# Moving the convolution units of a fused conv and ELU kernel to every fourth step, between the two groups' output turns

## The chip, the cores and the metric

The kernel runs on one core of a Trainium2 chip. The metric is the device time of one execution in microseconds (us), taken over several runs. Engines: PE is TensorE, ACT is ScalarE, DVE is VectorE, POOL is GpSimd, SP is SyncE.

## The reference, cut to what matters

```python
# x: (8, 4096, 192), weight: (8 heads, 7 taps)
w = softmax(weight, axis=-1)
out[b, s, h, :] = sum_k w[h, k] * x_pad[b, s + k, h, :]   # causal, 7 taps, 24 channels a head
h = out.reshape(32768, 192) @ w_in                        # (192, 2048)
g = where(h > 0, h, exp(min(h, 0)) - 1)                   # ELU
y = g @ w_out                                             # (2048, 192)
```

The result must be the float32 array of shape (32768, 192).

## The kernel before

The 32768 tokens are cut into 32 blocks of 1024, and each block's 2048 hidden channels into 16 slices of 128. One slice is a **step**, so a **stage** of 16 steps handles one block. The array of PE is split into two row tiles of 64 rows, which work side by side on different instructions. In each step a row tile does three kinds of work:

- one *h unit*: three matmuls 64x512 into a PSUM bank of its own. ACT then takes the exponential (line 752), POOL clamps it (705), DVE combines both into the ELU (868) and thereby frees the bank;
- two *output turns*, one for each group of 512 tokens: four matmuls 64x192 each into that group's accumulator. Both row tiles add to the same accumulator, so they must take turns, with a semaphore between them;
- in four of the 16 steps also its half of a *conv unit*: two matmuls 64x240 for two heads of a later block. Row tile 0 opens the bank, row tile 1 completes it, and ACT evacuates it (748).

```python
O_AT = (12, 16)              # first step of the accumulators of group 0 and group 1
CONV_AT = (14, 18, 23, 25)   # steps of a block's four conv units, from two stages ahead
X_AT = ((2, 1, 1), (1, 1, 0))   # the x loads: with the third unit half 1, with the second half 0
ZERO_AT = 8                  # POOL clears six rows here, in every fourth stage
...
    for n in range(LIVE, NP):
        ...
        for m in convs:
            lists[0] += c_items(m, 0)
        lists[0] += block_items(n, 0, 0) + block_items(n, 1, 0) + h_items(n, 0)
        lists[1] += h_items(n, 1)
        for m in convs:
            lists[1] += c_items(m, 1)
        lists[1] += block_items(n, 0, 1) + block_items(n, 1, 1)
        emit(lists)
```

`lists[rt]` is the order of one row tile's work within a step. `emit` merges the two lists into PE's single instruction stream by a clock of nominal durations. PSUM has eight banks. Two hold accumulators, and the others go round between h units and conv units: whoever needs a bank is given the one that the plan expects to come free first. Accumulators change every eight steps: group 0 at steps 12, 20, 28 and group 1 at 16, 24, 32 of the count in which the units stand at 14, 18, 23, 25.

```python
def take_bank(what, rt):
    if what not in bank_of:
        b = min(range(NBANK), key=lambda b: freed[b])
        ...
```

A finished block of conv results is transposed by a DMA from SP (`att<-csb`) and must have landed before the first h matmul of its stage. The x loads cast from float32 to bfloat16 and are issued from POOL, in the midst of POOL's stream of clamps. Which clamp they precede follows from the step of the conv unit that they are tied to.

## Time and profile before

| | before |
|---|---|
| time, median of 6 runs | 722.83 us |
| profiled span | 721.0 us |
| a stage of 16 steps, mean of 29 (steps 32 to 495) | 21.836 us |
| the same from the matmuls' pitches alone | 21.74 us |
| waits on each row tile, per stage | 0.105 us |
| waits on each row tile in the first 32 steps | 7.4 and 7.3 us |

The last four rows come from the start times of the matmul records, paired with the kernel's issue order, so that each row tile's own sequence is seen. The *wait* of a matmul is the distance from the start before it on that row tile, less the nominal pitch of that earlier matmul: 0.2158, 0.0825 or 0.1025 us.

### The profile page before, as it was taken

How to read it: one execution, taken by the hardware profiler on the slowest of the kernel's cores; microseconds unless marked ns; L12 is line 12 of the kernel's file. 1: busy time of each engine (PE TensorE's matmuls, PEld its weight loads, DVE VectorE, ACT ScalarE, POOL GpSimd, SP SyncE). 2: the span in 40 equal slices, each digit the busy share in tenths (PEclk: the TensorE clock that was granted, in tenths of full speed). 3: DMA queues.
4: the chain of work that ended last, by engine and by line, in shares of the span. 5: the costliest groups of instructions: out<-in, count | busy, mean ns of one | idle time of the engine just before them, and what ended most of it. 6: DMA issues, size and time to landing. Idle time of an engine off the chain costs nothing.

```text
span 721.0 us, 27609 instructions
## 1 busy us (share of the span) xinstructions
PE 713.7 (99%) x11846; PEld 673.2 (93%) x11847; DVE 642.9 (89%) x1048; ACT 678.4 (94%) x1289; POOL 667.7 (93%) x1112
## 2 busy tenths in 40 slices
PE   8999999999999999999999999999999999999997
PEld 4689999999999999999999999999999999999997
DVE  7999898998898998999888989988989988999993
ACT  6999999999999999999999999999999999999993
POOL 9989999999999999999999999999999999999893
PEclk9999999999999999999999999999999999999999
DMA  9725353555254664354553455652445553644212
GB/s 178 113 59 87 61 84 75 95 87 86 51 96 72 94 90 70 66 91 78 87 97 58 77 78 93 86 94 46 93 75 96 87 69 66 98 73 83 71 35 68
DMA packets 132303, 58.75 MB, mean 81 GB/s; under 512 B 98374, under 2 KB 131604, under 8 KB 132180
## 3 DMA queue, kind: packets, MB, share of 16 engines
q1 hardware_dynamic: 88388, 39.32, 23.7%
q0 software_dynamic: 43504, 16.77, 22.6%
q8 instruction: 93, 1.52, 0.9%
q10 hardware_dynamic: 288, 0.88, 0.3%
q14 instruction: 30, 0.25, 0.1%
HBM read 34.63 MB, written 25.46 MB: 83 GB/s over the span
## 4 chain that ended last, share of the span: by engine, by line
PE 95%; POOL 2%; DVE 1%; ACT 1%; issue 0%; DVEq 0%; POOLq 0%
PE H L1029 54%; PE H L1006 38%; PE H L981 4%; DVE gT L868 1%; POOL xg L622 1%; ACT E L752 1%; POOL w_in L642 0%; POOL w_out L653 0%; ACT csb L748 0%; POOL E L705 0%; POOL owner L670 0%; ACT osb L759 0%; DVE osb L859 0%; POOL block L680 0%; POOL ident L659 0%
## 5 line engine op out<-in xcount | busy, mean ns | idle before, releaser
L868 DVE SCALAR_TENSOR_TENSOR gT<-E,H 128x512 f16<-128x512 f32 x1024 | 633.1, 682 | 63.3 <-POOL E L705 61.2
L1029 PE MATMUL H<-w_out,gT 64*128 64x192 f16 x8192 | 681.7, 243 | 0.1
L1006 PE MATMUL H<-att,w_in 64*128 64x512 bf16 x3072 | 679.5, 376 | 0.8 <-DVE gT L868 0.6
L1029 PEld LDWEIGHTS H<-w_out,gT 64*128 64x128 f16 x8192 | 622.8, 94 | 24.7 <-PE H L1029 1.4
L705 POOL TENSOR_SCALAR E<-E 128x512 f32<-128x512 f32 x1024 | 607.0, 613 | 40.3 <-ACT E L752 29.8
L752 ACT ACTIVATE E<-H 128x512 f32<-128x512 f32 x1024 | 592.9, 602 | 26.3 <-PE H L1006 1.2
L1006 PEld LDWEIGHTS H<-att,w_in 64*128 64x128 bf16 x3072 | 275.6, 93 | 7.8 <-issue 1.4
L981 PE MATMUL H<-xg,Tm 64*128 64x240 bf16 x496 | 91.2, 263 | 0.2 <-DVE gT L868 0.2
L748 ACT ACTIVATE csb<-H 112x480 bf16<-112x480 f32 x124 | 70.0, 565 | 0.1
L759 ACT ACTIVATE osb<-H 128x384 f32<-128x384 f32 (+1 forms) x129 | 62.3, 485 | 6.8 <-PE H L1029 6.8
L622 POOL DMA_DIRECT2D xg<-in_x_dram x62 | 55.3, 902 | 0.2 <-issue 0.2
L981 PEld LDWEIGHTS H<-xg,Tm 64*128 64x128 bf16 x496 | 43.7, 94 | 4.6 <-DVE gT L868 0.8
L859 DVE COPY osb<-H 128x192 f32<-128x192 f32 x1 | 0.4, 358 | 7.3 <-PE H L1029 7.3
L903 PE MATMUL H<-zw 128*128 128x512 bf16 x10 | 3.8, 531 | 1.2 <-DVE zw L767 1.2
L957 PE MATMUL H<-xT,taps 128*128 128x256 bf16 (+1 forms) x23 | 3.7, 314 | 0.2 <-issue 0.2
L727 ACT ACTIVATE xb<-xs 128x512 bf16<-128x512 f32 x3 | 1.7, 618 | 2.2 <-DMA xs<-in_x_dram 2.2
L642 POOL DMA_DIRECT2D w_in<-in_moe_w_in_dram x6 | 3.6, 626 | 0.0
L957 PEld LDWEIGHTS H<-xT,taps 128*128 128x128 bf16 x24 | 2.2, 97 | 1.5
L903 PEld LDWEIGHTS H<-zw 128*128 128x128 bf16 x10 | 1.0, 122 | 2.6 <-DVE zw L767 1.2
L653 POOL DMA_DIRECT2D w_out<-in_moe_w_out_dram x3 | 2.7, 939 | 0.0
L720 ACT ACT_TABLE_LOAD x1 | 1.3, 1283 | 1.2 <-PEq L1096 1.2
L929 PEld LDWEIGHTS H<-ident,xb 64*64 64x64 bf16 x48 | 1.4, 129 | 1.1 <-ACT xb L727 1.1
(43 smaller groups left out, 20.7 us busy)
## 6 DMA issues: line engine op xcount, KB each, us to landing
out_dram<-osb SPq DMA_DIRECT2D x126, 192.0 KB, 3.3
xg<-in_x_dram POOLq DMA_DIRECT2D x61, 240.0 KB, 5.1
xs<-in_x_dram ACTq DMA_DIRECT2D x1, 768.0 KB, 4.5
w_in<-in_moe_w_in_dram POOLq DMA_DIRECT2D x3, 192.0 KB, 5.7
att<-csb SPq DMA_TRANSPOSE x31, 4.5
w_out<-in_moe_w_out_dram POOLq DMA_DIRECT2D x2, 192.0 KB, 9.1
w_out<-in_moe_w_out_dram POOLq DMA_DIRECT2D x1, 384.0 KB, 13.4
conv_band<-wband SPq DMA_DIRECT2D x1, 288.0 KB, 7.0
```

The costliest lines, as they stand in the source:

```text
L622: g.dma_start(xg[0:rows, b, 2 * w0 + gr : 2 * w1 : 2, :], src).then_inc(s_x[b][gr], 16)
L642: g.dma_start(w_in[0:HP, j, c0:c1], bass.AP(tensor=moe_w_in.tensor, offset=8 * j * FF + c0, ap=[[CPH * FF, HEADS], [FF, 8], [1, c1 - c0]], ...
L705: g.tensor_scalar(out=E[:, i % NE, :], in0=E[:, i % NE, :], scalar1=1.0, scalar2=0.0, op0=ALU.min, op1=ALU.max,).then_inc(s_clp)
L748: a.activation(*conv_evac(W, m), ACT.Copy).then_inc(s_ce)
L752: a.activation(E[:, i % NE, :], H[:, bank_of[item], :], ACT.Exp).then_inc(s_exp)
L759: a.activation(*out_evac(W, *item[1:]), ACT.Copy).then_inc(s_oev[item[2]])
L868: v.scalar_tensor_tensor(out=gT[:, s % NG3, q, u, :], in0=E[:, i % NE, :], scalar=1.0, in1=H[:, bank_of[item], :], op0=ALU.subtract, op1=A ...
L903: pe.matmul(H[:, bank, :], zw[:, 0:P], zw[:, 0:GS], start=True, stop=True)
L957: ins = pe.matmul(H[:, bank_of[item] + half, c0:c1], taps[:, tap, :], xT[:, j, HALO - PAD + tap + c0 : HALO - PAD + tap + c1], start=(tap ...
L981: ins = pe.matmul(H[:, bank_of["c", m], 256 * q : 256 * q + UC], Tm[rows, h, :], xg[rows, s % NXB, :, CPH * h : CPH * (h + 1)].rearrange(" ...
L1006: ins = pe.matmul(H[:, bank_of[item[:3]], :], w_in[HP * r : HP * (r + 1), j, FC * q : FC * (q + 1)], att[HP * r : HP * (r + 1), s % 2, j, ...
L1029: ins = pe.matmul(acc_of(k, g)[:, D * kb : D * (kb + 1)], gT[HP * rt : HP * (rt + 1), t % NG3, q, g, t0 : t0 + P], w_out[HP * rt : HP * (r ...
```

## The change

The intent is to have the accumulators' changes and the conv units never compete for a bank: a unit every four steps, two steps from any change, and in its step at the place where the two groups' turns meet.

```diff
 O_AT = (12, 16)
-CONV_AT = (14, 18, 23, 25)
+CONV_AT = (14, 18, 22, 26)
+CONV_POS = ((4, 4), (4, 4), (4, 4), (4, 4))
+POS_FROM = 30
...
-        lists = [[], []]
-        convs = conv_steps.get(n, [])
-        for m in convs:
-            lists[0] += c_items(m, 0)
-        lists[0] += block_items(n, 0, 0) + block_items(n, 1, 0) + h_items(n, 0)
-        lists[1] += h_items(n, 1)
-        for m in convs:
-            lists[1] += c_items(m, 1)
-        lists[1] += block_items(n, 0, 1) + block_items(n, 1, 1)
+        blocks = [[block_items(n, g, rt) for g in range(2)] for rt in range(2)]
+        lists = [sum(blocks[0], []) + h_items(n, 0), h_items(n, 1) + sum(blocks[1], [])]
+        for m in conv_steps.get(n, []):
+            for rt, later in enumerate(CONV_POS[m % CU] if n >= POS_FROM else (0, 0)):
+                later += 3 * rt
+                lists[rt][later:later] = c_items(m, rt)
         emit(lists)
```

Two more edits (`E_DVE` tested by half and group, `EVAC_LAG = 0.0`) do nothing with the values given and are left out. The x loads move with the units that they are tied to: from steps 18 and 23 to 18 and 22.

More of the change, by code (lines that the diff above doesn't have):

```diff
@@ L51 @@
 E_DVE = ()
+EVAC_LAG = 0.0
 HELD = {"h": 2900.0, "c": 1300.0, "a": 1400.0}
@@ L384, in bass_lightweight_conv__then__act_elu_kernel @@
                 what = ("e",) + item[1:3]
-                if item[2] in E_DVE or item[1:3] == (NK - 1, 1):
-                    dve_order.append((at + AHEAD, what))
+                if (item[1] % 2, item[2]) in E_DVE or item[1:3] == (NK - 1, 1):
+                    dve_order.append((at + AHEAD + EVAC_LAG, what))
                 else:
```

## The prediction

> **What bounds the kernel now.** I read the page first: busy shares (part 1), costliest groups (part 5).
>
> ```profile
> PE 713.7 (99%) x11846; PEld 673.2 (93%) x11847; DVE 642.9 (89%) x1048; ACT 678.4 (94%) x1289; POOL 667.7 (93%) x1112
> ...
> L1029 PE MATMUL H<-w_out,gT 64*128 64x192 f16 x8192 | 681.7, 243 | 0.1
> L1006 PE MATMUL H<-att,w_in 64*128 64x512 bf16 x3072 | 679.5, 376 | 0.8 <-DVE gT L868 0.6
> ...
> L981 PE MATMUL H<-xg,Tm 64*128 64x240 bf16 x496 | 91.2, 263 | 0.2 <-DVE gT L868 0.2
> L748 ACT ACTIVATE csb<-H 112x480 bf16<-112x480 f32 x124 | 70.0, 565 | 0.1
> ...
> L622 POOL DMA_DIRECT2D xg<-in_x_dram x62 | 55.3, 902 | 0.2 <-issue 0.2
> ```
>
> PE is busy nearly always, in two row tiles of 64 rows that run side by side, so "99%" hides whether both tiles are full. The durations 243 and 376 ns are pipelined records; what counts is the pitch on one row tile. The chain of work that ended last, in order of time, gives it, since it is PE work almost throughout:
>
> ```profile
> 131.13 0.27 PE H L1006 x2
> 132.64 0.25 PE H L1006 x2
> 152.97 0.27 PE H L1006 x2
> ...
> 174.81 0.27 PE H L1006 x2
> ...
> 658.28 0.25 PE H L1006 x2
> 659.59 0.25 PE H L1006 x2
> 660.90 0.25 PE H L1006 x2
> 662.21 0.27 PE H L1006 x2
> ```
>
> Three things are to be seen. A step without a conv unit takes 1.31 us (658.28 to 659.59 to 660.90). A step with one takes 1.51 us (131.13 to 132.64). The pattern repeats every 21.84 us (131.13, 152.97, 174.81), which is one stage of 16 steps with four conv units.
>
> Next I took every matmul start from the timeline of PE, paired it with the kernel's own issue order, and formed pitches per row tile: 0.2158 us after an h matmul (64x512), 0.0825 after an output matmul (64x192), 0.1025 after a conv matmul (64x240). Per row tile a step is 3 x 0.2158 + 8 x 0.0825 = 1.3075 us, and a conv unit adds 2 x 0.1025 = 0.205. A full stage is 16 x 1.3075 + 4 x 0.205 = **21.74 us**. Measured is 21.84: only **0.10 us of 21.84** is waiting. This is the whole prize in the steady part. Where a pitch exceeds its nominal value shows who loses it, the same in each of 29 stages (steps 32 to 495): row tile 0 waits 0.033 us for the conv unit's bank at step 23 of the schedule (7 mod 16) and 0.050 for the bank of the second group's accumulator that opens at step 24; row tile 1 waits 0.019 inside step 24 and 0.050 at the h unit of step 26. The units at 14 and 18 lose under 0.005 each. One such stage in the timeline of PE:
>
> ```profile
> 456.91 0.38 PE L1006 MATMUL H<-att,w_in 64*128 64x512 bf16 x1
> 456.92 0.41 PE L1029 MATMUL H<-w_out,gT 64*128 64x192 f16 x3
> 457.13 0.38 PE L1006 MATMUL H<-att,w_in 64*128 64x512 bf16 x1
> ...
> 457.72 0.47 PE L1029 MATMUL H<-w_out,gT 64*128 64x192 f16 x3
> ```
>
> The h matmuls of row tile 0 start 0.22 apart; three output matmuls take 0.41 when they flow (456.92) and 0.47 where the opening accumulator waited (457.72). Who kept the bank is seen in ACT's timeline at the same place:
>
> ```profile
> 457.32 0.56 ACT L748 ACTIVATE csb<-H 112x480 bf16<-112x480 f32 x1
> ...
> 458.25 0.50 ACT L759 ACTIVATE osb<-H 128x384 f32<-128x384 f32 x1
> ...
> 460.19 0.56 ACT L748 ACTIVATE csb<-H 112x480 bf16<-112x480 f32 x1
> ...
> 463.05 0.48 ACT L759 ACTIVATE osb<-H 128x384 f32<-128x384 f32 x1
> ```
>
> ACT evacuates a conv unit (csb), an accumulator (osb) and a conv unit within 2.9 us, then nothing of the kind for 2.4 us. By the issue plan the accumulator that opens at step 24 is given the very bank that the conv unit of step 23 has just left.
>
> **What the Trainium skill says.** "TensorE: Matmul & The Clock Gate", part 1, gives a warm start-to-start pitch of N / 2.4 GHz plus about 2.5 ns, so 215.8, 82.5 and 102.5 ns at N = 512, 192 and 240; this trace agrees on each row tile to within 1 ns, so nothing can make the matmuls themselves faster. "TensorEngine Tiling (Array Packing)", Gotcha 1, says that two row tiles may not use one PSUM bank at once and that software must keep them apart; that is why the two row tiles take turns at an accumulator and at a conv bank. In the trace 0.318 us between the end of one tile's turn and the other's start costs nothing, as steps without conv are exactly 1.3075. "Perfetto Trace Analysis", Optimization Strategy, says that the same gap repeated on the engine that should be full can mean PSUM has too few buffers; the trace agrees: 0.05 us at the same places of each stage, each at a bank. The same page, "DMA Instruction — SWDGE (GPSIMD)", says that a load issued from GpSimd has its descriptors made there; here each x load takes 902 ns of POOL.
>
> **The change part by part.** Nothing is added or removed. The E_DVE test and EVAC_LAG are inert, as E_DVE is empty and the lag zero.
>
> (a) Conv units 23 and 25 go to 22 and 26. Accumulators change at steps 12, 20, 28 (first group) and 16, 24, 32 (second), so all four units then sit two steps from a change, as 14 and 18 do now. The waits above should go: 0.033 + 0.050 on one row tile, 0.019 + 0.050 on the other. The row tiles' mean total of waits is 0.105 us per stage, but 0.24 of the 29 stages' 3.04 is a single late bank near 281 us. I expect 0.01 a stage to stay: 29 x (0.105 - 0.010) = **-2.75 us**.
>
> (b) From step 30 each unit's two matmuls are inserted between the two groups' turns: on row tile 0 after 4 x 0.0825 = 0.33 us instead of at the start, on row tile 1 after the h unit and the first turn (0.978) instead of after the h unit (0.648). Turn gaps: first group 0.33 to 0.648, second 0.865 to 1.183, both 0.318, the gap that is free now. The conv bank is taken 0.33 later, apart from the h bank taken at the start of the step. ACT's evacuation hardly moves: it now ends about 1.16 us after the last conv matmul's start (459.59 to 460.75) because it stands behind an h unit's exponential; 0.33 later ACT is just free. Cost 0, value within (a).
>
> (c) The start: steps 16 to 23 still lose 1.7 us to banks that come late out of the start-up backlog, and step 23 to 24 some 0.2 for the reason in (a). The conv at 22 comes one step nearer to the backlog. I count -0.1, uncertain by 0.3.
>
> Sum: 722.84 - 2.75 - 0.1 = **719.9 us** (-0.4%).
>
> **The rivals.** (1) *The transpose becomes late.* The last unit of a stage must be evacuated, transposed by DMA and landed before the next stage's first h matmul at step 32. Landing times, from the tile att:
>
> ```profile
> DMA to landing us min/median/max: 3.9/4.5/5.6
> ```
>
> Today it lands 1.96 to 3.7 us ahead of need (stages 2 to 31). The change takes away a step (1.31) and 0.33 within the step, and gives back about 0.3 at ACT: 0.6 is left in the worst stage. If each landing keeps its time, no stage waits. Against: the store of the accumulator that ends at step 27 is issued 2.65 us after the transpose now and would follow after some 1.3 us, and the slow landings today are those that overlap it. For: the x load and the other store, which overlap its first half now, would be mostly done. If a third of the stages came 0.3 us late, the time would be 29 x 1/3 x 0.3 = 2.9 us longer, 722.8: no gain.
>
> (2) *POOL takes over.* The second x load is issued after the third conv unit, so it moves from step 23 to 22, nearer to the first at 18. POOL's E instructions come every 0.6075 us when back to back (4.86 for 8), 1.215 of each 1.3075 step; of a load's 0.90 only 4 x 0.0925 + 0.205 = 0.58 is worked off in four steps. POOL carries 0.3 us into the second load, against 0.23 or less now.
>
> ```profile
> DVE gT L868 <- POOL E L705: 57.7, 135, 0.9
> ```
>
> DVE waits for POOL already (window 60 to 680), for which PE shows almost nothing. After the load at 18 the next accumulator opens with 0.46 us of bank slack and the h units of step 19 with 0.3; 0.3 of carry could use the latter up. If it costs 0.05 a stage: +1.45 us, 721.4. A bound it cannot be: 32 x 0.6075 + 2 x 0.90 = 21.24 per stage, under 21.74.
>
> (3) *Waits are all gone, at the start as well*: 722.84 - 3.04 - 1 = 718.8. Nothing in the plan frees the start, so I doubt it.
>
> **Range and chances.** The floor is 718.8; the usual misses are upward, by POOL (721.4) or the transpose (about 722). I take 719.0 to 721.9. The possible gain is under 0.6%, and slower by 2% would need 14 us, 0.5 us in every stage, which no rival makes: faster 0.005, same 0.985, slower 0.01.
>
> **What would show it.** Right: the chain repeats every 21.74 to 21.75 us instead of 21.84, output matmuls in threes take 0.41 where an accumulator opens, and csb and osb alternate on ACT at intervals of about 2.7 us. (b) is right if a conv step still takes 1.51. Rival 1 would show as PE waits on the DMA that writes att at the first h matmul of a stage; rival 2 as longer DVE waits for POOL and a gap on PE two to four steps after the second x load. Wrong would be a period of 21.80 or more, or any loss at steps 16 to 30 above 0.3 us.

## The result and the profile after

The changed kernel takes 720.7 us (median of 6 runs, 720.16 to 721.13) against 722.83 us. The ratio is 0.9966, with a 95% interval of 0.9953 to 0.9979. Ratios here are the mean time of one kernel's fast runs over that of the other's in the same rounds, so they are not quite the ratio of the medians quoted. By the rule of 2% the class is "same", and the small gain is clear of the noise. The profiled span fell from 721.0 to 718.9 us.

The page after, parts 1 and 5 (busy us, share, instructions; then groups with busy time and mean ns):

```profile
PE 712.0 (99%) x11847; PEld 683.3 (95%) x11847; DVE 641.5 (89%) x1048; ACT 678.5 (94%) x1289; POOL 664.4 (92%) x1112
...
L1006 PE MATMUL H<-att,w_in 64*128 64x512 bf16 x3072 | 680.8, 376 | 0.7 <-DVE gT L868 0.5
L1029 PE MATMUL H<-w_out,gT 64*128 64x192 f16 x8192 | 680.7, 243 | 0.1
...
L981 PE MATMUL H<-xg,Tm 64*128 64x240 bf16 x496 | 90.9, 263 | 0.2 <-DVE gT L868 0.2
L748 ACT ACTIVATE csb<-H 112x480 bf16<-112x480 f32 x124 | 70.8, 571 | 0.1
...
L622 POOL DMA_DIRECT2D xg<-in_x_dram x62 | 55.3, 896 | 0.2 <-issue 0.2
```

The page hardly moves: the same instructions of the same length, each engine as busy as before. A gain of 0.3% in a kernel that is bound throughout by one engine can't be seen in shares. It can be seen in the pitch. Lines of the chain that ended last, in order of time, after:

```profile
68.35 0.27 PE H L1006 x2
155.43 0.27 PE H L1006 x2
242.53 0.27 PE H L1006 x2
...
329.76 0.27 PE H L1006 x2
416.86 0.27 PE H L1006 x2
```

Before, such pieces came in every stage, 21.84 us apart. Now, apart from a disturbed stage near 281 us, they come only in every fourth: 155.43 - 68.35 = 87.08 us, a quarter of which is 21.77. From the matmul records, the mean stage is 21.769 us (nominal 21.74), and the waits per stage are 0.038 us instead of 0.105. They are not spread evenly. Three stages in four have 0.002 and 0.017 us on the two row tiles, that is nothing. Every fourth stage has 0.09 to 0.15 on row tile 0, mostly at the h unit of step 26, and the stage near 281 us has 0.19.

ACT's timeline after, for one stage (start, duration, operation), evacuations only:

```profile
481.97 0.57 ACT L748 ACTIVATE csb<-H 112x480 bf16<-112x480 f32 x1
...
483.44 0.48 ACT L759 ACTIVATE osb<-H 128x384 f32<-128x384 f32 x1
...
487.41 0.57 ACT L748 ACTIVATE csb<-H 112x480 bf16<-112x480 f32 x1
...
489.54 0.49 ACT L759 ACTIVATE osb<-H 128x384 f32<-128x384 f32 x1
```

Conv units (csb) and accumulators (osb) now alternate strictly, 1.5 to 4.0 us apart; the burst of three within 2.9 us is gone. What is special about every fourth stage stands in POOL's timeline after:

```profile
499.07 0.89 POOL L622 DMA_DIRECT2D xg<-in_x_dram  x1
500.00 1.77 POOL L705 TENSOR_SCALAR E<-E 128x512 f32<-128x512 f32 x3
501.71 0.25 POOL L637 MEMSET xg<- 6x192 bf16 x1
501.93 4.15 POOL L705 TENSOR_SCALAR E<-E 128x512 f32<-128x512 f32 x7
```

POOL issues the second x load (0.89 us), does three clamps, and then clears six rows (0.25 us). It clears in every fourth stage, for a block that begins a new sequence. Clamps pile up while POOL does such other work; this backlog is called POOL's *debt* below. At 503.31, row tile 0's h unit of step 26 waited 0.112 us for its bank. Two more lines of the profile after belong to the rivals. The first is the row for DVE's waits on POOL (total us, times, longest), in the list of waits from 60 to 680 us; the second is the landing times of the transposes, from the tile att:

```profile
DVE gT L868 <- POOL E L705: 55.1, 116, 0.9
```

```profile
DMA to landing us min/median/max: 3.8/3.8/5.8
```

The accounts close. On each row tile the waits of the 29 stages fell from 3.04 to 1.10 us, and those of the first 32 steps from 7.37 to 7.17 (means of the two row tiles): 1.94 + 0.20 = 2.14 us, against 722.83 - 720.7 = 2.13 measured.

### The profile page after: what moved, and what is told of

Same layout as the page of the kernel before. It is cut to its first block, busy times and chain, and to the rows that moved or that the text cites. A ratio compares the mean times of both kernels' runs of the same rounds, so it can differ in the third digit from the quotient of the medians.

```text
span 718.9 us, 27610 instructions
## 1 busy us (share of the span) xinstructions
PE 712.0 (99%) x11847; PEld 683.3 (95%) x11847; DVE 641.5 (89%) x1048; ACT 678.5 (94%) x1289; POOL 664.4 (92%) x1112
## 4 chain that ended last, share of the span: by engine, by line
PE 95%; POOL 2%; DVE 1%; ACT 1%; issue 0%; DVEq 0%; POOLq 0%
PE H L1029 54%; PE H L1006 37%; PE H L981 4%; DVE gT L868 1%; POOL xg L622 1%; ACT E L752 1%; POOL w_in L642 0%; POOL w_out L653 0%; ACT csb L748 0%; POOL E L705 0%; POOL owner L670 0%; ACT osb L759 0%; DVE osb L859 0%; POOL block L680 0%; POOL ident L659 0%
## 5 line engine op out<-in xcount | busy, mean ns | idle before, releaser
L1029 PE MATMUL H<-w_out,gT 64*128 64x192 f16 x8192 | 680.7, 243 | 0.1
L1029 PEld LDWEIGHTS H<-w_out,gT 64*128 64x128 f16 x8192 | 608.5, 94 | 16.4 <-PE H L1029 1.6
L752 ACT ACTIVATE E<-H 128x512 f32<-128x512 f32 x1024 | 585.4, 601 | 24.0 <-PE H L1006 1.0
L981 PE MATMUL H<-xg,Tm 64*128 64x240 bf16 x496 | 90.9, 263 | 0.2 <-DVE gT L868 0.2
L981 PEld LDWEIGHTS H<-xg,Tm 64*128 64x128 bf16 x496 | 42.5, 94 | 1.2 <-DVE gT L868 0.5
L733 ACT ACTIVATE w_in<-w_in 64x1536 bf16<-64x1536 bf16 (+1 forms) x2 | 2.3, 1162 | 0.0
```

The lines of the kernel that those rows point to most:

```text
L752: a.activation(E[:, i % NE, :], H[:, bank_of[item], :], ACT.Exp).then_inc(s_exp)
L981: ins = pe.matmul(H[:, bank_of["c", m], 256 * q : 256 * q + UC], Tm[rows, h, :], xg[rows, s % NXB, :, CPH * h : CPH * (h + 1)].rearrange(" ...
L1029: ins = pe.matmul(acc_of(k, g)[:, D * kb : D * (kb + 1)], gT[HP * rt : HP * (rt + 1), t % NG3, q, g, t0 : t0 + P], w_out[HP * rt : HP * (r ...
```

## The experiments

Twelve kernels were run, in three batches of four (a to d, e to h, i to l, the last on another chip), all but two with correct results. The kernel before was timed again in each batch (722.77, 722.86 and 723.0 us), and the ratios are to that. "Waits" are per row tile and stage (mean of row tiles and of 29 stages, steps 32 to 495). "Stage" is the mean length of those stages.

| kernel | time, us | ratio to before | waits, us | stage, us |
|---|---|---|---|---|
| before | 722.83 | | 0.105 | 21.836 |
| after | 720.7 | 0.9966 | 0.038 | 21.769 |
| a: steps 22 and 26 alone | 725.94 | 1.0045 | 0.234 | 21.964 |
| b: placing alone | 723.14 | 1.0008 | 0.106 | 21.839 |
| c: after, loads eight steps apart | 720.19 | 0.9965 | 0.019 | 21.751 |
| d: after, clearing at step 12 | 720.05 | 0.9964 | 0.022 | 21.754 |
| e: before, loads nine steps apart | 726.09 | 1.0048 | 0.219 | 21.950 |
| f: after, units on the changes | 750.63 | 1.0383 | 1.062 | 22.792 |
| g: after, c and d together | 720.24 | 0.9961 | 0.019 | 21.752 |
| h: after, both loads at once | 740.55 | 1.0248 | 0.728 | 22.459 |
| i: a without later loads (wrong result) | 720.16 | 0.9961 | 0.010 late | |
| j: before without later loads (wrong result) | 721.22 | 0.9977 | 0.064 late | |
| k: placing on row tile 1 alone | 733.87 | 1.0156 | 0.492 | 22.224 |
| l: units after both turns | 732.04 | 1.0126 | 0.439 | 22.170 |

For i and j, "late" is a typical stage once the loads have ended.

### The two halves of the change, each alone (a, b)

```diff
 # a_units_only, from the changed kernel
-POS_FROM = 30
+POS_FROM = 9999
 # b_place_only, from the changed kernel
-CONV_AT = (14, 18, 22, 26)
+CONV_AT = (14, 18, 23, 25)
```

> The changed kernel without its placing inside the step (units stay at the head of row tile 0's list and behind row tile 1's h unit, as before; only the steps 22 and 26 are new). My theory: the steps alone bring the gain, since it is the accumulator between the units of 23 and 25 that waited; waits of 0.02 to 0.05 us a stage, a stage of about 21.77, time 720.4 to 721.0. Rival (the placing between the two turns is what frees the bank): waits stay at 0.08 or more a stage and the time at 721.8 or more.

> The changed kernel with the units back at steps 14, 18, 23, 25, but placed between the two groups' turns. My theory: the crowding about step 24 stays, so 0.07 to 0.12 us of waits a stage, a stage of 21.81 to 21.85, time 721.8 to 723. Rival (the placing matters): waits below 0.05 a stage, time near 720.7.

Kernel a came out at 725.94 us, 0.45% *slower* than before. My theory had put it at 720.4 to 721.0. The rival's "0.08 or more" and "721.8 or more" hold, but it spoke of old waits that stay, not of new ones. Kernel b came out level with before (interval 0.9994 to 1.0021). So each half alone gains nothing, the first alone costs 3.2 us, and together they gain 2.1. My theory that the new steps alone bring the gain fell here. The list of waits of PE's weight loads, 60 to 680 us, first in the kernel before and then in a:

```profile
PEld H L981 <- DVE gT L868: 0.2, 1, 0.2
```

```profile
DVE gT L868 <- POOL E L705: 56.8, 142, 0.9
...
PEld H L981 <- DVE gT L868: 8.5, 53, 0.4
```

In a, the conv matmul (L981) waits 53 times for a bank that DVE frees, nearly twice in each of 29 stages; before, once in the whole window. By the matmul records these are the units at steps 22 and 26, with 0.11 and 0.10 us of their own. The units at 14 and 18 do not wait. With the 0.01 us that follows each, they are nearly the whole of row tile 0's 0.234. Row tile 0's wait then cuts into the time between the row tiles' turns (0.235 us in a's steps without a unit, by the records), and row tile 1's first turn of the same step waits 0.08 us each time, until 0.220 us have passed. That is most of row tile 1's share.

Why 22 and 26, and not 14 and 18? They are the units that come four steps after an x load (18 and 22). The plan gives each of the four units the bank of row tile 0's h unit of three steps before; for the units at 22 and 26 that is the h unit one step after a load, which POOL clamps late. Experiment e makes the same point by accident.

### Is POOL behind the waits that were left, and those of before? (c, d, e, h)

```diff
 # c_loads_apart, from the changed kernel; e_before_loads_apart: the same edit on the kernel before
-X_AT = ((2, 1, 1), (1, 1, 0))
+X_AT = ((2, 1, 1), (0, 1, 0))
 # d_zero_later, from the changed kernel
-ZERO_AT = 8
+ZERO_AT = 12
 # g_both: c and d
 # h_loads_together, from the changed kernel
-X_AT = ((2, 1, 1), (1, 1, 0))
+X_AT = ((1, 1, 1), (1, 1, 0))
```

> The changed kernel with the first x load of a stage issued at the unit of step 14 instead of 18, so that the two loads are eight steps apart on POOL. My theory of what is left (1.10 us of waits in 29 stages, nearly all in the stages in which POOL also clears six rows and in the one in which its load came 0.15 us late: POOL's debt from two loads four steps apart): the waits fall to under 0.01 a stage, time about 1 us lower, 719.6 to 719.9. Rival (the units' places and the banks leave it): 720.7, unchanged.

> The changed kernel with POOL's clearing of six rows (0.25 us, every fourth stage) moved from step 8 to step 12 of the stage, when POOL has worked off the second load. My theory: the 0.08 to 0.13 us of waits in every fourth stage go; only the stage near 281 us keeps some 0.18; total of waits in steps 32 to 495 falls from 1.10 to about 0.3 us, time about 719.9. Rival: nothing moves, as the fourth stages differ by something else (the batch's first load, for one).

> The changed kernel with both the loads eight steps apart and the clearing at step 12. My theory: no more than the better of the two alone, as both remove the same debt; waits under 0.1 us in all 29 stages, a stage of 21.74, time 719.5 to 719.8. It is the version that should beat both kernels.

> The changed kernel with both x loads issued one behind the other at the unit of step 18, so that POOL's debt is 1.8 us at once. My theory (POOL's debt is what is left of the waits): banks come late after step 18, 0.3 to 1 us a stage, a stage of 22.0 or longer, time 728 or more. Rival (PE doesn't feel POOL): unchanged, 720.7.

> The kernel before with its x loads at the units of steps 14 and 23 instead of 18 and 23. It asks whether the 0.105 us a stage that the kernel before lost was due to the bank between the two close units (my theory) or to POOL's debt from two loads five steps apart (rival). My theory: 0.07 to 0.11 us a stage stay, as the accumulator of step 24 still takes the bank that the unit of 23 just left; time 722 to 723. Rival: waits below 0.03 a stage, time near 720.

In c, the waits of the 29 stages fell from 1.10 us to 0.55 and 0.57 on the two row tiles. DVE's waits for POOL, in the same list as above, fell to 62 of at least 0.15 us, where the changed kernel has 116:

```profile
DVE gT L868 <- POOL E L705: 46.5, 62, 1.0
```

Of the seven fourth stages, six still lose some 0.06 us each on row tile 0. In d, they lose next to nothing (0.03 or less), and what is left is mainly the stage near 281 us. There POOL's first load of the stage began 0.15 us late, in the kernel before and the changed one, in c and in d; why is not known. Both edits confirm that the rest was POOL's. The expected total for d was 0.3; it was 0.63 and 0.65, of which 0.5 on row tile 1 is the 0.017 a stage that is no wait. With g nothing more is gained, as expected (0.50 and 0.59), but my forecast of less than 0.1 us of waits and 719.5 to 719.8 us was missed.

The times of c, d and g (720.19, 720.05, 720.24) lie 0.5 us below the changed kernel's 720.7, as the waits say they should. But the changed kernel was timed in other rounds, and the intervals of all four ratios overlap almost wholly. So these three beat the kernel before, while their advantage over the changed kernel is shown in the traces and not in the times. My forecasts for c, a gain of 1 us and waits under 0.01 us a stage (0.019 measured), were too good.

In h, the two loads stand back to back, and POOL's delay is 1.8 us at once:

```profile
DVE gT L868 <- POOL E L705: 71.5, 137, 1.8
...
PEld H L1006 <- DVE gT L868: 11.5, 28, 0.6
PEld H L981 <- DVE gT L868: 7.7, 28, 0.3
```

An h unit waits once and the conv unit once in 28 of the 29 stages. The time is 740.55 us, 2.5% more than before. The loads are the same and POOL has no more to do in all; that they come together instead of four steps apart is enough.

Experiment e was to tell two causes of the old 0.105 us apart, and met neither: it became slower, 726.09.

```profile
PEld H L981 <- DVE gT L868: 4.3, 26, 0.4
```

The conv unit now waits once a stage, and the matmul records put it at step 18: 0.16 us, again exactly four steps after the load that I had just moved to step 14. The older waits at 24 and 26 stayed (0.04 and 0.05). So this edit added a new wait instead of showing what the old ones were. It left the suspicion that a unit at the head of a step four steps after a load meets POOL's debt. That called for loads that are absent, not moved.

### Loads taken away (i, j)

```diff
 # i_units_only_no_loads from a; j_before_no_loads from the kernel before
+LOADED = 6
 ...
-            z_count += s % SPB == 0 and s > 0
+            z_count += s % SPB == 0 and 0 < s <= LOADED
-                x_count[s % NXB][g] += 16 * (s > 0)
+                x_count[s % NXB][g] += 16 * (0 < s <= LOADED)
 ...
+                if s > LOADED and gr < 2:     # in load_x
+                    return
 ...
+                if s > LOADED:                # in batch_zeros
+                    return
```

The result is wrong (relative error 1.25), as the later blocks compute on old x.

> The slow kernel of units moved without their placing, with no x loads and no clearing on POOL after sequence block 6 (the later blocks compute on old x: the result is wrong on purpose). The question is why the moved units at the head of a step waited 0.11 us for a bank at steps 22 and 26. New theory: a unit four steps after an x load meets POOL's debt from that load, which makes every h bank come late; without loads the stages from the 7th on lose under 0.02 us and last 21.74. Rival: taking a bank in the same moment as the h unit of the other row tile is too early whatever POOL does; then 0.15 us or more a stage stay.

> The kernel before with no x loads and no clearing after block 6 (wrong on purpose). The question is what part of its 0.105 us a stage was POOL's. Theory of the prediction (the accumulator of step 24 takes the bank that the unit of 23 has just left): the 0.05 at that accumulator stays, so 0.05 to 0.1 us a stage in the later stages. New theory (POOL's debt makes banks late, and close units only meet it): under 0.02 us a stage.

In i, the same kernel a that lost 0.234 us a stage loses 0.002 and 0.017 in a typical stage as soon as the loads end: no waits. (One later stage, near 302 us, lost 0.12 us, and some of the last 0.02 to 0.06; why is not known.) The list of waits has three entries left, in the stages that still load (the inserted lines shift the line numbers by 5):

```profile
PEld H L986 <- DVE gT L873: 0.5, 3, 0.2
```

So the whole cost of the moved units came with the loads. The edit takes the loads' DMA traffic away as well; that it is POOL's time is read from its lag, the time from the end of ACT's exponential to the start of POOL's clamp. At the h units whose banks the units of 22 and 26 get, the lag is 0.34 and 0.48 us in a and 0.08, no lag, in i (medians). The rival, that the head of a step is too early in itself, fell. It was not far off, though: in i the unit at step 22 starts 0.09 to 0.24 us after the DVE operation that frees its bank has ended, where 0.057 is what a waiting unit shows, so as little as 0.04 us is to spare even with an undisturbed POOL.

The same measure shows what the placing adds. In a, the units of 22 and 26 start 0.057 us after their bank came free, which is to say that they waited. In the changed kernel they get the banks of the same h units and start 0.24 and 0.15 us after (medians).

In j, the kernel before still loses 0.064 us a stage without loads: 0.05 at the accumulator of step 24 and 0.019 behind it, every time. The waits at the unit of step 23 (0.03) and at the h unit of step 26 (0.04) are gone. The accumulator starts 0.055 us after ACT has evacuated the unit of 23, again the time of one that waited. The one such wait that is long enough for the list names that evacuation:

```profile
PEld H L1034 <- ACT csb L753: 0.2, 1, 0.2
```

So about 0.064 of the old 0.105 was the bank handed from the unit of 23 to the accumulator of 24, as the prediction had it, and 0.04 was POOL's.

How POOL's debt runs off can be read from POOL's lag in the changed kernel, here at the h units of row tile 1 (medians of 29 stages, us; 0.08 is no lag):

```
step of the schedule   18    19    20    21    22    23    24    25    26    27
POOL's lag             0.08  0.63  0.42  0.32  0.17  0.72  0.32  0.41  0.25  0.14
```

The load tied to step 18 shows from step 19 on and is nearly worked off by step 22, when the next one starts. The second makes the h banks late into step 26, which is where the changed kernel waits if 0.25 us of clearing is added.

### Where in the step, and where in the stage (k, l, f)

```diff
 # k_tile1_only, from the changed kernel
-CONV_POS = ((4, 4), (4, 4), (4, 4), (4, 4))
+CONV_POS = ((0, 4), (0, 4), (0, 4), (0, 4))
 # l_after_turns
+CONV_POS = ((8, 8), (8, 8), (8, 8), (8, 8))
 # f_on_changes
-CONV_AT = (14, 18, 22, 26)
+CONV_AT = (12, 16, 20, 24)
```

> The changed kernel with only row tile 1's half of each unit placed between the turns; row tile 0's half is at the head of the step again, so the bank is taken 0.33 us earlier. New theory (it is the later taking of the bank that pays): as slow as the units moved alone, 0.2 us or more of waits a stage, time 725 or more. Rival (the gain is in the turns of row tile 1 or in the evacuation): near 720.7.

> The changed kernel with the units after both turns of their step: the bank is taken 0.33 us later still, and row tile 1's half ends the step. If taking later is all that counts, waits of at most 0.04 us a stage and a time of 720 to 720.8. If the place between the turns is needed (the unit's evacuation then falls together with the exponentials of two h units, which end at the same time), the waits rise to 0.1 us or more a stage and the time to 722 or more.

> The changed kernel with its units at steps 12, 16, 20, 24: just as evenly spread, but in the very steps in which an accumulator opens. If the distance from the accumulators' changes is what counts (my theory), the waits are above 0.1 us a stage and the stage is 21.84 or longer, time 722.5 or more; if only the even spacing of four steps counts (rival), the stage stays near 21.77 and the time near 720.7. The start-up differs here too, so the stage length is what decides.

Kernel k is as slow as foretold, and slower than a, but it proves less than it was meant to. The unit at step 22 waits 0.16 us for its bank again, so taking it at the head of the step does cost. But waits of 0.055 to 0.06 us also stand at units 14 and 18, where no bank is late. There the edit cuts the time between the row tiles' turns at the first group, as row tile 0's turn is put off by the 0.205 of the conv half, and row tile 1's is not: from 0.37 us, measured in k's steps without a unit, to 0.165. Row tile 1 waits until 0.220 have passed. I had overlooked that. The two causes are mixed in k.

Kernel l takes the conv bank 0.33 us later still and is worse, so later is not simply better. At the units of 22 and 26, row tile 0's h unit now waits 0.18 us: its bank is needed only 0.205 us after the conv unit's. And row tile 1's half ends the step, as does row tile 0's h unit. The exponential of row tile 1's next h unit (steps 23 and 27) then starts 0.54 us after the nominal end of its matmuls instead of 0.20. In the list of waits ACT starves in turn; in the changed kernel this row is absent:

```profile
ACT E L752 <- PE H L1006: 35.3, 112, 0.6
```

Between the turns, the conv bank is needed 0.33 us after one h bank and 0.53 us before the next.

Kernel f, evenly spaced but in the steps at which accumulators change (its loads move along, to steps 16 and 20), loses 1.06 us a stage, ten times what the kernel before lost:

```profile
PEld H L1006 <- ACT osb L759: 17.9, 54, 0.4
PEld H L1029 <- DVE gT L868: 11.8, 54, 0.4
PEld H L981 <- DVE gT L868: 9.0, 28, 0.3
```

Now h units wait for an accumulator's evacuation (osb), opening accumulators (L1029) for a bank of DVE's, and the conv unit as well. So even spacing alone is not enough. That the distance from the accumulators' changes is what counts fits these waits; f changes that distance together with the place of the loads, still four steps apart.

## Why the prediction was right or wrong, point by point

**The time and the class** were right: 720.7 us lies in 719.0 to 721.9. The sum as written, 722.84 - 2.75 - 0.1, comes to 719.99 and not to 719.9, so the miss of the point is 0.7 us.

**The bound and the size of the prize** were right. No kernel's mean stage came below the 21.74 us worked out from the pitches, and conv steps still take 1.513 us on row tile 0. The gain and the 2.14 us of waits removed agree to 0.01 us.

**Where the waits came from** was right for 0.064 of 0.105 us: the accumulator of step 24 (j). The 0.04 around it were put down to the same crowding and were POOL's.

**Step (a) failed as put.** "All four units then sit two steps from a change, as 14 and 18 do now. The waits above should go" was to bring -2.75 us by the steps alone. Alone they bring +3.2 us (a). What was missed is that 14 and 18 have another advantage besides their distance from a change: no x load lies four steps before them. The units at 22 and 26 follow the loads of 18 and 22, and POOL's debt then makes every h bank late (i).

**Step (b) failed with it.** "Cost 0, value within (a)" is right on the cost: b alone has 0.106 us a stage against 0.105. The value is not within (a). Taking the bank 0.33 us later in the step outlasts POOL's debt and turns the loss of a (0.234 us a stage) into 0.038. Neither part is worth anything without the other, and a sum of parts could not say so. That the total came right is in part luck: (a) was some 6 us too good (-2.75 forecast, +3.2 measured), and (b), put down as 0, brought 5.2 us on top of it (725.94 to 720.7).

**The rest assumed to stay** was mis-sized: 0.010 us a stage was assumed, 0.038 measured, so 29 x 0.028 = 0.81 us. Less the 0.10 us by which the start did better than forecast, that is the whole miss. Rival 2 had named the cause (POOL's carry from two loads four steps apart), its place ("two to four steps after the second x load") and a size of 0.05 a stage. It had not counted the 0.25 us clearing on POOL, so it expected the cost in each stage instead of every fourth. Its other sign, longer DVE waits for POOL, did not come (57.7 before, 55.1 after).

**Step (c)**: -0.1 forecast, -0.20 measured in the first 32 steps, within the 0.3 allowed.

**Rival 1, the late transpose,** did not occur. The 30 later stages had the block 0.17 to 2.4 us ahead of need, where the worst was put at 0.6. The worst is the last stage, with a landing time of 5.8 us; so there is no room to move the last unit a step further. The median landing time fell from 4.5 to 3.8 us. The stores' overlap, which I had feared, did not lengthen it.

**The spacing on ACT** was right in the alternation and wrong in the "about 2.7 us": it varies from 1.5 to 4.0, as the two groups' turns end at different points of a step. (The pause after the old burst was 2.30 us, 460.75 to 463.05, and not 2.4.)

**The gap between turns**, "in the trace 0.318 us", is the sum of nominal pitches. By the records row tile 1's turn begins 0.23 to 0.29 us after row tile 0's has ended in the kernel before, and 0.29 to 0.30 in the changed one, without waits. So the argument of (b) holds: placing the units there costs nothing at the turns.

**"Within 1 ns"** of the page's pitch is right but for the second conv matmul on row tile 1, which shows 107 ns instead of 102.5.

## What to carry to other kernels

When an engine is full and its last waits are for buffers, look for what holds the buffers longest at that moment; here it was an engine two hand-overs downstream that had been interrupted for 0.9 us four steps earlier. Estimate the parts of a scheduling change together, or test each alone: a move that is harmful by itself can be the right one once the request for the buffer is shifted within its step. Look at everything that interrupts a nearly full engine, and not only at the work that was seen to wait: bunched loads cost 2.5% (h). Moving them apart helped in c and harmed in e, where the moved load came just ahead of a buffer's request, so check what each interruption then precedes.

## What the Trainium skill lacked or had wrong

- "Perfetto Trace Analysis", section Optimization Strategy: it says that consistent bubbles can mean too few buffers. Here the same bubbles went without a buffer more, when POOL, on which the return of the buffers depends, was left undisturbed (waits of 0.234 us a stage in a, none in a typical stage of i). That paragraph doesn't name this second cause.
- "Perfetto Trace Analysis", section DMA Instruction — SWDGE (GPSIMD): it says that the descriptors are made on GpSimd, without the effect on compute in the same stream. Here each 240 KB load held POOL for 896 ns (mean), with clamps lagging by 0.63 us one step and 0.32 us three steps later (medians; 0.08 is no lag), and two loads back to back cost 2.5% of the kernel's time.
- "TensorEngine Tiling (Array Packing)", Gotcha 1: it asks for synchronization between row tiles and gives no time for it. Here a turn that had to wait for the other row tile's began 0.220 us after that one's end (a, e and k), and turns 0.23 us apart did not wait.
- "TensorE: Matmul & The Clock Gate", section Back-to-back issue gap: it says that in a stream of weight loads and matmuls the formula N / 2.4 + 2.5 over-counts at large N (some 131 ns at N = 512) and under-counts at small N. Here such a stream, one weight load to each matmul, kept to the formula on each row tile within 1 ns: 215.8 ns at N = 512 and 82.5 at N = 192, with the two row tiles side by side. The page doesn't say how its stream was laid out in the array.
- Belonging to no page: the median landing time of the transpose fell from 4.5 to 3.8 us when its issue moved by a step; the runs don't show the cause.
